# Half of one batch's q load moved behind four DMA transposes, and two key tiles rectified on VectorE, in a linear-attention and routed-MoE kernel

## The chip, the core and the metric

The kernel runs on one core of one Trainium2 chip. The metric is the device time of one execution in microseconds, as a median over runs. A NeuronCore has TensorE (PE, matmuls; PEld is its weight load), VectorE (DVE), ScalarE (ACT), GpSimd (POOL) and the sync engine (SP). Each takes its instructions in the order in which they were written. Work between engines is ordered by semaphores alone. Sixteen DMA engines move data for all queues; here POOL issues the loads from HBM, and SP issues the transposing copies.

## What is computed

The reference has two parts. The first is a linear attention over 8 batches of 8 heads, 576 positions and a head size of 64; the second a mixture of 8 experts, whose gate is balanced by 8 rounds of row and column normalisation.

```python
r = np.maximum(x, 0.0)                       # phi: of q and of k
phi = np.concatenate([r * c, r * s], -1)     # c, s: cos, sin of the position
kv  = np.einsum('bhsf,bhsd->bhfd', k_p, v)
z   = np.sum(k_p, axis=2)
num = np.einsum('bhsf,bhfd->bhsd', q_p, kv)
den = np.einsum('bhsf,bhf->bhs', q_p, z)[..., None] + 1e-06
x   = num / den                              # (4608, 512) over all heads
...
h = np.maximum(x @ w1[e], 0.0)               # for each expert e
out += P[:, e:e+1] * (h @ w2[e])             # P: the balanced gate
```

## The kernel before

The first 170 us or so hold the attention, with expert 0 laid between its pieces so that TensorE always has matmuls to do. The rest is the balancing and experts 1 to 7. The change is in the attention part.

One batch is handled as four pairs of heads, `hk` 0 to 3. In what follows (b, hk) is the pair hk of batch b, and batches count from 0, so the "second batch" is b = 1 and the "fourth" b = 3. A load (`load`, L201) brings one half of a batch, that is two pairs, of q, k or v: 288 KB, issued on POOL's queue, into one of four buffers for each name. With `held_back` the load also waits for the last VectorE instruction written before it.

For each pair the following is done:

- `prep_k` rectifies k in place, on ACT or, with `by_scalar=False`, on DVE. `prep_kp` multiplies it by cos and sin (DVE, `k_p`), and `prep_v` copies v next to a column of ones (DVE or ACT; the destination is borrowed room in `acc_lo`).
- `prep_q` rectifies q (DVE, `q_ld`) and multiplies it by cos and sin into one of three `q_p` buffers (DVE). From batch 2 on, a DMA transpose (L360, on SP's queue) then writes `q_pT`. For batches 0 and 1, TensorE transposes in `turn`.
- `sums` makes kv and z on PE (`small_ps<-acc_lo,k_p`), and its results are copied by ACT (`kv_sb`) and DVE (`zsel`).
- `denominators` multiplies all four transposed q of a batch by `zsel` on PE, 24 short matmuls, pair after pair. DVE then makes `den`, its reciprocal, `hi` and `hl`.
- `attend` spreads `hl` on PE (into `small_ps`), ACT copies it to `rb`, PE makes the numerator, and DVE multiplies the two into `xT`. There are four `small_ps` banks, and one `attend` uses four. So the second spread of the next `attend` waits for ACT to have read the last one, and its numerator waits for DVE's `xT`.

Expert 0 runs over blocks `j` of 512 tokens with 16 slots each: 8 slots of the first matmul (`ffn1`, `h_ps`, ACT writes `hT`) and 8 half slots of the second (`ffn2`, `y_ps`, ACT copies to `acc_lo`). A table written by hand, `at(block, slot, fn, ...)`, lays the attention's steps behind the slots; nothing reorders it. Block 0 finishes batch 1 and prepares the q of batch 2. Block 1 computes the sums, denominators and `attend` of batch 2, and prepares batch 3. Ahead of the blocks, a loop over `hk` runs `attend(0, hk)` between the first matmuls of expert 0 and prepares batch 1's k.

What the change touches, by the profile's line numbers: the first loop (L625 to L643), the loads of batch 3 (block 0, slot 13: L673 and L674; block 1, slot 0: L683 to L685) and the table of batch 3's preparation in block 1 (L704 to L708), put in place at L717. The k and v loads of batch 3 already stand at block 1, slot 0, behind the DVE work of that slot.

In block 1 the order on ACT around the change is: `hT` of slot 7, the two `k_ld` of (3,0) and (3,1), the copy of `y_ps`, and then the `rb` copies of `attend(2, 0)`. The order on DVE is: `q_ld` and `q_p` of (3,0), (3,1) and (3,2), then `den` to `hl` of batch 2, then `xT`.

Of the kernel before, what the change touches and what calls it, by code (L numbers as in the profile page):

```python
# [25 lines left out]
def kernel(  # L26
# [91 lines left out]
    te, ve, se = bound  # L118
# [62 lines left out]
    with ExitStack() as p1:  # L181
# [156 lines left out]
        def prep_k(b, hk, by_scalar=True):  # L338
            k16 = loaded["k", b, hk]
            if b and by_scalar:  # L340
                se.activation(out=k16, in_=k16, func=AF.Relu)
            else:
                ve.tensor_scalar(out=k16, in0=k16, scalar1=0.0, scalar2=None, op0=ALU.max)
# [27 lines left out]
        def prep_kp(b, hk):  # L371
            k16 = loaded.pop(("k", b, hk))
            k_p = kp_pool.tile([P, C, 2, D], F16, name="k_p")
            ve.tensor_tensor(
                out=k_p[:], in0=k16.unsqueeze(2).to_broadcast([P, C, 2, D]),
                in1=cs, op=ALU.mult,
            )
            kps[b, hk] = (
                k_p, v_augs[(b * HK + hk) % len(v_augs)] if b else loaded.pop(("v", b, hk))
            )  # L380
# [146 lines left out]
        def attend(b, hk):  # L527

            parts = ((0, 2 * C3), (2 * C3, C))
            rb_ps = [ps_s.tile([P, 512], FP32, name="small_ps") for _ in parts]  # L530
            rb = rb_pool.tile([P, C * HP], FP32, name="rb")
            for i, (c0, c1) in enumerate(parts):
                for j in range(c0 // C3, c1 // C3):
                    te.matmul(
                        out=rb_ps[i][:, (j * C3 - c0) * HP : ((j + 1) * C3 - c0) * HP],
                        lhsT=spread[0:96, j, hk].rearrange("p hh d -> p (hh d)"),
                        rhs=hls[b][:],
                        start=True,
                        stop=True,
                    )  # L540
                se.copy(out=rb[:, c0 * HP : c1 * HP], in_=rb_ps[i][:, 0 : (c1 - c0) * HP])
            num_ps = [ps_s.tile([P, 512], FP32, name="small_ps") for _ in parts]
            for i, (c0, c1) in enumerate(parts):
                for hh in range(2):
                    te.matmul(
                        out=num_ps[i][hh * HP : (hh + 1) * HP, 0 : (c1 - c0) * HP],
                        lhsT=kvs[b][0][:, hk, hh, :],
                        rhs=qTs[b, hk][:, c0:c1, hh * HP : (hh + 1) * HP],
                        start=True,
                        stop=True,  # L550
                    )
                ve.tensor_tensor(
                    out=xT[:, hk, b * S + c0 * HP : b * S + c1 * HP],
                    in0=num_ps[i][:, 0 : (c1 - c0) * HP],
                    in1=rb[:, c0 * HP : c1 * HP],
                    op=ALU.mult,
                )
# [25 lines left out]
        def at(block, slot, fn, *args):  # L583
            todo.setdefault((block, slot), []).append((fn, args))
# [39 lines left out]
        ]  # L624
        for hk in range(HK):  # L625
            attend(0, hk)
            if hk == 3:
                prep_k(1, 3)
            for kt in ((), (0,), (1,), (2, 3))[hk]:
                for ft, h_ps in enumerate(first_ps):  # L630
                    te.matmul(
                        out=h_ps[:],
                        lhsT=w0[0][:, kt, ft * P : (ft + 1) * P],
                        rhs=xT[:, kt, 0:TCH],
                        start=(kt == 0),
                        stop=(kt == KT - 1),
                    )
                    if kt == KT - 1:
                        se.activation(out=hT[:, ft, 0:TCH], in_=h_ps[:], func=AF.Relu)
            for i in ((), (0,), (1, 2), ())[hk]:  # L640
                prep_k(1, i)
            for i in ((), (0,), (1,), (2, 3))[hk]:
                prep_kp(1, i)  # L643
        for hk in range(3):
            prep_q(1, hk)

        for j in range(B):
            b = j + 1
            if j == 0:

                def sums_first(half):
                    sums_made(1, half, sums_begun(1, half))

                for hk in range(HK):
                    for i in range(3):
                        at(0, (5, 6, 6, 7)[hk], turn, 1, hk, i, i != 1)
                    if hk == 0:
                        at(0, 5, prep_q, 1, 3)
                    if hk == 2:
                        at(0, 6, prep_v, 1, 0, se.copy)  # L660
                        at(0, 6, prep_v, 1, 2, ve.tensor_copy)
                    if hk == 3:
                        at(0, 7, prep_v, 1, 1, se.copy)
                        at(0, 7, prep_v, 1, 3, ve.tensor_copy)
                for half in range(2):
                    at(0, 7, sums_first, half)
                at(0, 8, denominators, 1)
                at(0, 10, gates, 0)
                for hk in range(HK):
                    at(0, 11 + hk, attend, 1, hk)  # L670
            elif b < B:
                if j == 1:
                    for half in range(2):  # L673
                        at(0, 13, load, b + 1, half, "q", True)  # L674
                    for hk in range(HK):
                        if hk >= 2:
                            at(j, 0, prep_k, b, hk, False)
                        at(j, 0, prep_kp, b, hk)
                        at(
                            j, (0, 0, 1, 3)[hk], prep_v, b, hk,  # L680
                            (ve.tensor_copy, se.copy)[hk // 2],
                        )
                    for name in "kv":  # L683
                        for half in range(2):
                            at(j, 0, load, b + 1, half, name, True)  # L685
                    at(j, 3, sums, b, 0)
                    at(j, 5, sums, b, 1)
                else:
                    at(j, 0, sums, b, 1)
                at(j, 6 if j == 1 else 3, denominators, b)  # L690
                for hk in range(HK):
                    at(j, (9, 10, 12, 13)[hk] if j == 1 else 6 + 2 * hk, attend, b, hk)
            if j:
                at(j, 5, gates, j)
            if j == 0:
                for half in range(2):
                    at(j, 3, load, b + 1, half)
                for slot, fn, hk, *args in (
                    (8, prep_q, 0), (11, prep_k, 0), (12, prep_q, 1), (12, prep_k, 1),
                    (13, prep_q, 2), (14, prep_q, 3),  # L700
                ):
                    at(j, slot, fn, b + 1, hk, *args)
            elif b + 1 < B:
                for slot, fn, hk in (  # L704
                    (4, prep_q, 0), (5, prep_q, 1), (5, prep_q, 2), (7, prep_k, 0),
                    (8, prep_k, 1), (10, prep_kv, 0), (10, prep_k, 2), (12, prep_q, 3),
                    (12, prep_kv, 1), (12, prep_k, 3), (13, prep_kv, 2), (14, prep_kv, 3),
                ) if j == 1 else (  # L708
                    (4, prep_q, 0), (5, prep_k, 0), (5, prep_q, 1), (6, prep_k, 1),
                    (7, prep_q, 2), (8, prep_kv, 0), (8, prep_k, 2), (9, prep_q, 3),  # L710
                    (10, prep_k, 3), (10, prep_kv, 1), (12, prep_kv, 2), (13, prep_kv, 3),
                ) if j == 2 else (
                    (3, prep_k, 0), (4, prep_q, 0), (4, prep_k, 1), (5, prep_q, 1),
                    (7, prep_kv, 0), (7, prep_k, 2), (7, prep_q, 2), (9, prep_q, 3),
                    (9, prep_k, 3), (9, prep_kv, 1), (11, prep_kv, 2), (13, prep_kv, 3),
                ):
                    at(j, slot, fn, b + 1, hk)  # L717
                at(j, 15 if j == 1 else 14, sums, b + 1, 0)
            if j == 1:
                for name in "qkv":  # L720
                    for half in range(2):
                        at(j, 12, load, b + 2, half, name, True)
            elif j and b + 2 < B:
                for half in range(2):
                    at(j, 11 + half, load, b + 2, half, "qkv", True)
# [438 lines left out]
    for e in range(1, E):  # L1164
        if e == 2:
            se = nc.scalar
# [49 lines left out]
    while stream:  # L1216
        _, pair, name = stream.pop(0)
# [32 lines left out]
```

## Time and profile before

| what | value |
|---|---|
| median of 6 runs | 983.25 us (982.97 to 984.49) |
| the profiled execution | 982.97 us, span 981.3 us |
| PE busy | 966.2 us, 98% of the span |
| DVE busy | 806.7 us, 82% |
| ACT busy | 565.6 us, 58% |
| POOL busy | 60.7 us, 6% |
| granted TensorE clock | 1.0 |
| loads of q, 16 issues of 288 KB | median 6.6 us from issue to landing |
| loads of k, 16 issues of 288 KB | median 7.9 us |
| transposes into `q_pT`, 18 issues | median 3.8 us |
| PE's longest wait for a DMA | 1.7 us, once, for `q_pT<-q_p` |

The span is the time from the first to the last profiled instruction, and 1.7 us of the execution lie around it. The first five of the page's 40 slices, of 24.5 us each, show the DMA engines busy for nine tenths or more and the sixth for eight; later slices show seven tenths at most.

### The profile page before, as it was taken

How to read it: one execution, taken by the hardware profiler on the slowest of the kernel's cores; microseconds unless marked ns; L12 is line 12 of the kernel's file. 1: busy time of each engine (PE TensorE's matmuls, PEld its weight loads, DVE VectorE, ACT ScalarE, POOL GpSimd, SP SyncE). 2: the span in 40 equal slices, each digit the busy share in tenths (PEclk: the TensorE clock that was granted, in tenths of full speed). 3: DMA queues.
4: the chain of work that ended last, by engine and by line, in shares of the span. 5: the costliest groups of instructions: out<-in, count | busy, mean ns of one | idle time of the engine just before them, and what ended most of it. 6: DMA issues, size and time to landing. Idle time of an engine off the chain costs nothing.

```text
span 981.3 us, 20268 instructions
## 1 busy us (share of the span) xinstructions
PE 966.2 (98%) x7871; PEld 674.0 (69%) x7871; DVE 806.7 (82%) x1833; ACT 565.6 (58%) x1263; POOL 60.7 (6%) x82
## 2 busy tenths in 40 slices
PE   9999999989999999999999999999999999999997
PEld 6544454457777777777777777777777777777775
DVE  6767774789889888988788888988888888988887
ACT  6766665467776555555555555555555555555551
POOL 6221110010000000000000000000000000000001
PEclk9999999999999999999999999999999999999999
DMA  9999981740113400223103400223103401104435
GB/s 162 185 158 166 152 139 21 146 70 33 42 33 68 92 25 25 57 62 68 49 25 68 92 25 26 63 58 66 48 25 72 89 25 34 41 26 119 127 87 129
DMA packets 80336, 73.54 MB, mean 75 GB/s; under 512 B 33264, under 2 KB 72176, under 8 KB 80240
## 3 DMA queue, kind: packets, MB, share of 16 engines
q0 software_dynamic: 27232, 30.94, 20.2%
q1 hardware_dynamic: 52768, 41.06, 17.1%
q8 instruction: 61, 1.00, 0.4%
q14 instruction: 35, 0.29, 0.1%
q10 hardware_dynamic: 240, 0.26, 0.1%
HBM read 83.12 MB, written 12.98 MB: 98 GB/s over the span
## 4 chain that ended last, share of the span: by engine, by line
PE 92%; DVE 3%; DMA 2%; ACT 2%; POOL 1%; issue 1%; POOLq 0%; DVEq 0%; ACTq 0%; SPq 0%
PE rows_ps L109 34%; PE h_ps L109 27%; PE copied_ps L109 11%; PE p_ps L109 11%; PE y_ps L109 5%; PE small_ps L109 3%; DMA q_pT<-q_p 1%; DMA k_ld<-in_k_dram 1%; ACT hT L109 0%; DVE den L109 0%; DVE xT L109 0%; DVE acc_hi L923 0%; POOL hs_last L938 0%; DVE P_tok L109 0%; DVE k_p L109 0%
## 5 line engine op out<-in xcount | busy, mean ns | idle before, releaser
L923 DVE SCALAR_TENSOR_TENSOR acc_lo<-rows_ps,P_tok,acc_lo 128x512 f32<-128x512 f32 (+1 forms) x322 | 203.1, 639 | 74.8 <-PE rows_ps L109 74.7
L109 PEld LDWEIGHTS <-H 128*128 128x128 f16 x2080 | 203.0, 98 | 83.1 <-issue 1.2
L859 ACT CAST u<-h_ps 128x384 f16<-128x384 f32 x288 | 137.8, 478 | 131.1 <-PE h_ps L109 131.1
L109 PEld LDWEIGHTS <-w1e 128*128 128x128 f16 x1632 | 156.5, 98 | 66.5 <-issue 6.4
L853 DVE CUSTOM_DVE_ANT_0 H<-p_ps,u 128x384 f16<-128x384 f32 x329 | 180.8, 550 | 6.7 <-PE p_ps L109 6.5
L109 PEld LDWEIGHTS <-hs 128*128 128x128 f16 x1500 | 146.6, 98 | 56.2
L109 PE MATMUL h_ps<-S,w1e 128*128 128x384 f16 x672 | 164.1, 326 | 1.1 <-ACT u L109 0.9
L109 PE MATMUL p_ps<-xT,T 128*128 128x384 f16 x672 | 164.1, 326 | 0.1
L109 PE MATMUL rows_ps<-V,H 128*128 128x256 f16 x1000 | 150.0, 273 | 0.7 <-DVE acc_hi L923 0.7
L109 PE MATMUL h_ps<-xT,w1e 128*128 128x384 f16 (+1 forms) x616 | 150.0, 350 | 0.2 <-DVE xT L109 0.2
L109 PE MATMUL rows_ps<-w2e,hs 128*128 128x256 f16 x1000 | 150.0, 273 | 0.0
L891 ACT ACTIVATE H<-h_ps 128x384 f16<-128x384 f32 x144 | 70.7, 491 | 95.0 <-PE h_ps L109 95.0
L109 PEld LDWEIGHTS <-T 128*128 128x128 f16 x1008 | 98.1, 98 | 29.2 <-issue 2.7
L109 PE MATMUL rows_ps<-w2e,H 128*128 128x256 f16 (+1 forms) x568 | 91.2, 285 | 0.0
L872 ACT COPY copied_ps<-h_ps 128x384 f32<-128x384 f32 x144 | 67.5, 468 | 35.1 <-PE h_ps L109 35.1
L882 ACT ACTIVATE H<-copied_ps 128x384 f16<-128x384 f32 x144 | 70.9, 492 | 20.3 <-PE copied_ps L109 20.3
L109 PE MATMUL h_ps<-S,T 128*128 128x384 f16 x336 | 81.8, 325 | 0.3 <-ACT copied_ps L109 0.3
L109 PE MATMUL copied_ps<-xT,w1e 128*128 128x384 f16 x336 | 82.1, 326 | 0.0
L109 PE MATMUL copied_ps<-w2e,H 128*128 128x256 f16 x504 | 75.5, 272 | 0.0
L109 PE MATMUL rows_ps<-V,hs 128*128 128x256 f16 x500 | 75.0, 272 | 0.0
L923 DVE SCALAR_TENSOR_TENSOR acc_lo<-copied_ps,P_tok,acc_lo 128x256 f32<-128x256 f32 x126 | 60.0, 476 | 0.4
L923 DVE SCALAR_TENSOR_TENSOR acc_hi<-rows_ps,P_tok,acc_hi 128x512 f32<-128x512 f32 (+1 forms) x56 | 41.3, 737 | 20.5 <-PE rows_ps L109 19.7
(147 smaller groups left out, 948.8 us busy)
## 6 DMA issues: line engine op xcount, KB each, us to landing
S<-x_saved SPq DMA_DIRECT2D x108, 192.0 KB, 2.4
out_dram<-acc_lo SPq DMA_DIRECT2D x62, 128.0 KB, 2.4
w1e<-in_moe_w_dram POOLq DMA_DIRECT2D x7, 1024.0 KB, 8.9
w2e<-in_moe_w_dram POOLq DMA_DIRECT2D x7, 1024.0 KB, 9.7
q_ld<-in_q_dram POOLq DMA_DIRECT2D x16, 288.0 KB, 6.6
k_ld<-in_k_dram POOLq DMA_DIRECT2D x16, 288.0 KB, 7.9
v_ld<-in_v_dram POOLq DMA_DIRECT2D x16, 288.0 KB, 9.2
x_saved<-S SPq DMA_DIRECT2D x18, 192.0 KB, 1.9
```

The costliest lines, as they stand in the source:

```text
L109: i = getattr(self.engine, name)(*args, **kwargs)
L853: latest = ve._custom_dve(TENSOR_ADD_SAT, out=out, in0=ps[:, 0:TU], in1=t[:], s0=FP32_MAX, s1=0.0)
L859: se.copy(out=t[:], in_=ps[:, 0:TU])
L872: se.copy(out=Y[:, 0:TU], in_=X[:, 0:TU])
L882: se.activation(out=h11, in_=Y[:, 0:TU], func=AF.Relu)
L891: se.activation(out=h12, in_=X[:, 0:TU], func=AF.Relu)
L923: ve.scalar_tensor_tensor(out=a, in0=rows, scalar=P_tok[:, g, self.e : self.e + 1], in1=a, op0=ALU.mult, op1=ALU.add,)
```

## The change

Four things are edited.

- The q load of batch 3 at block 0, slot 13 brings only the first half, the pairs 0 and 1. The second half is issued at block 1, slot 0, ahead of the k and v loads there. So it comes after the last of batch 2's four transposes.
- In block 1 the preparation of q for (3,2) moves from slot 5 to slot 8. On DVE it then stands behind `den` to `hl` of batch 2.
- The copy of v for (3,3) at slot 14 goes from DVE to ACT.
- In the first loop (1,2) and (1,3) of k are rectified by DVE and no longer by ACT, and that of (1,3) is written later.

The instructions of PE and their order are the same in both kernels. SP issues the same transposes in the same order.

```diff
             attend(0, hk)
-            if hk == 3:
-                prep_k(1, 3)
...
             for i in ((), (0,), (1, 2), ())[hk]:
-                prep_k(1, i)
+                prep_k(1, i, i < 2)
             for i in ((), (0,), (1,), (2, 3))[hk]:
+                if i == 3:
+                    prep_k(1, i, False)
                 prep_kp(1, i)
...
                 if j == 1:
-                    for half in range(2):
-                        at(0, 13, load, b + 1, half, "q", True)
+                    at(0, 13, load, b + 1, 0, "q", True)
...
-                    for name in "kv":
-                        for half in range(2):
-                            at(j, 0, load, b + 1, half, name, True)
+                    for name, half in (("q", 1), ("k", 0), ("k", 1), ("v", 0), ("v", 1)):
+                        at(j, 0, load, b + 1, half, name, True)
...
-                    (4, prep_q, 0), (5, prep_q, 1), (5, prep_q, 2), (7, prep_k, 0),
+                    (4, prep_q, 0), (5, prep_q, 1), (7, prep_k, 0), (8, prep_q, 2),
                     (8, prep_k, 1), (10, prep_kv, 0), (10, prep_k, 2), (12, prep_q, 3),
-                    (12, prep_kv, 1), (12, prep_k, 3), (13, prep_kv, 2), (14, prep_kv, 3),
+                    (12, prep_kv, 1), (12, prep_k, 3), (13, prep_kv, 2), (14, prep_kp, 3),
+                    (14, prep_v, 3),
...
-                    at(j, slot, fn, b + 1, hk)
+                    at(j, slot, fn, b + 1, hk, *((se.copy,) if fn is prep_v else ()))
```

## The prediction

> **What bounds the kernel now.** I read the busy times first, then PE's waits, then the chain of waits around the transposes, then the timeline of 50 to 70 us. The busy times:
>
> ```profile
> PE 966.2 (98%) x7871; PEld 674.0 (69%) x7871; DVE 806.7 (82%) x1833; ACT 565.6 (58%) x1263; POOL 60.7 (6%) x82
> ```
>
> PE is busy for 98% of the span and its instructions don't change, so the change can only touch PE's idle time. PE's waits name one for a DMA, and the chain (start, length, what) passes through that transfer:
>
> ```profile
> PE small_ps L109 <- DMA q_pT<-q_p: 1.7, 1, 1.7
> ...
> 47.14 8.76 DMA q_pT<-q_p
> ...
> 55.98 0.76 DVE q_p L109
> 56.74 0.28 DVE den L109
> ```
>
> The transfer is the transpose of (2,3): issued at 47.14, landed at 55.90, where the median transpose takes 3.8 us. The q loads of batch 3 were issued in the same moments, so they shared the DMA engines with it. The timeline shows the rest (start, us, engine, shapes, in brackets the idle time and who ended it):
>
> ```profile
> 45.44 1.43 POOL L201 DMA_DIRECT2D q_ld<-in_q_dram  x2 [12.62 <-DVE q_p L109]
> 45.78 0.48 DVE L109 TENSOR_SCALAR q_ld<-q_ld 128x576 f16<-128x576 f16 x1
> ...
> 51.67 1.43 POOL L201 DMA_DIRECT2D k_ld<-in_k_dram  x2 [4.81 <-ACT hT L109]
> ...
> 55.02 0.31 DVE L109 TENSOR_SCALAR q_ld<-q_ld 128x576 f16<-128x576 f16 x1 [1.00 <-DMA q_ld<-in_q_dram]
> 55.93 0.35 PE L109 MATMUL small_ps<-q_pT,zsel 128*32 128x192 f16 x6 [1.72 <-DMA q_pT<-q_p]
> ...
> 57.28 0.60 ACT L109 ACTIVATE hT<-h_ps 128x512 f16<-128x512 f32 x1 [3.04 <-PE h_ps L109]
> 57.78 1.25 ACT L109 ACTIVATE k_ld<-k_ld 128x576 f16<-128x576 f16 x2
> ...
> 59.19 0.42 PE L109 MATMUL small_ps<-hl,acc_hi 96*128 96x192 f16 x3 [0.21 <-DVE hl L109]
> ...
> 60.07 0.82 DVE L109 TENSOR_TENSOR xT<-small_ps,rb 128x384 f16<-128x384 f32 x2 [0.94 <-ACT rb L109]
> ...
> 61.12 0.44 PE L109 MATMUL small_ps<-q_pT,kv_sb 128*64 128x384 f16 x4
> ...
> 69.81 0.46 PE L109 MATMUL small_ps<-acc_lo,k_p 64*128 64x65 f16 x18 [0.35 <-DVE acc_lo L109]
> ```
>
> PE idles 1.72 us at 54.21, 0.21 us before 59.19 and 0.35 us before 69.81: 2.28 us together. That is all the change can win here.
>
> **The change part by part, against this execution (982.97 us, span 981.3).**
>
> *The transpose of (2,3).* One load of the two goes from in front of it. Between 36 and 38 us loads alone move 210 GB/s, so 294,912 bytes are 1.40 us: landing at 54.5, a wait of 0.3 us left. The upper gain: in 53.50 to 54.20 the engines moved only 20 GB/s, an empty stretch that need not come again; with that the landing is at 53 or earlier. PE asks at 54.21, so 1.4 to 1.72 us come back. I take 1.72.
>
> *`prep_q` of (3,2) behind `hl`.* It now stands between PE's end at 56.18 and `den`, which started at 56.66 behind `q_p`. An earlier `den` began 0.04 us after its matmuls (36.00 to 36.04), so 0.44 us of the DVE chain go, and the wait of 0.21 us before 59.19 with them. Its own 0.31 + 0.76 us fit into DVE's 0.94 us of idle time before `xT`, nearly. So up to here PE is 1.72 + 0.21 = 1.93 us early.
>
> *What the moved load pushes back.* This decides. On POOL's queue the second q half now goes out ahead of k. Its last wait is the `k_p` that ends at 51.13, and POOL started 0.31 us after such an end in two other places (45.13 to 45.44, 66.97 to 67.28): 51.44, as against 51.67 for k before. The first k half follows 0.71 us later, at 52.15, second in line, and both v halves slip by half a microsecond. How long does a second load in line take? The trace has five:
>
> ```profile
> DMA to landing us min/median/max: 6.1/6.1/6.1
> ...
> DMA to landing us min/median/max: 6.4/6.4/6.4
> ...
> DMA to landing us min/median/max: 8.9/8.9/8.9
> ```
>
> These are the second loads issued at 67.99, 52.38 and 46.15; those at 85.63 and 106.14 took 6.3 and 5.7. The 8.9 had the transposes beside it, and so may this one, since SP issues (3,0) at 52.74. Bounds for the landing of k: 57.85 (5.7) and 61.05 (8.9). I take 6.05, between 5.7 and 6.4, so 58.2. Before, it landed at 51.67 + 5.3 = 57.0 and ACT took it at 57.78 without a wait.
>
> Behind that `k_ld` on ACT stand the second `k_ld`, the copy of `y_ps` and `rb`, without a gap: 57.78 to 60.07 is 2.29 us from `k_ld` to `xT`. The first half of `xT` takes 0.56 us and PE's numerator of (2,1) waits for it, with 0.05 us for the semaphore. So that numerator starts no earlier than landing + 2.90. In the kernel before it started at 61.12, held by PE itself. PE, 1.93 us early, asks at 59.19. With k at 58.2 it starts at 61.10: the whole gain is gone but 0.02 us, as ACT's wait for k has taken the place of PE's wait for the transpose. Each microsecond of k's landing is a microsecond of PE, from 56.3 (nothing lost) upward.
>
> The second q half itself is first in line; such loads took 4.1 to 6.1 us, so it lands at 55.5 to 57.5, and DVE wants it at 57.2. That costs 0 to 0.3 us, hidden under ACT's wait. The first v half, fourth in line, is wanted at about 63.1 and has landed by then if 9.6 us, the longest v load nearby, holds (53.6 + 9.6 = 63.2).
>
> *`prep_v` of (3,3) on ACT.* DVE sets the end of block 1: from the `xT` at 64.11 to the last v copy at 69.75 it hardly idles, and PE waits 0.35 us for that copy. Without it DVE ends with `k_p` at 69.39. ACT has 1.26 us idle before 67.46 and needs 0.70. Gain 0.35; without ACT's gap it would be nothing.
>
> *Two k on VectorE.* ACT loses two `k_ld` of 0.70 us. One stood at 23.50 with 0.52 us of idle time behind it, so worth nothing; the other delayed `rb` to 22.93 by some 0.15 us. DVE gains two operations, 0.30 us each by its k rows at 49.03 and 50.04. The first stands ahead of the `k_p` at 22.50, which overlaps it by 0.08 us as neighbours do here, so the `xT` that started at 23.44 after 0.18 us of idle time starts at 23.40 (-0.04). If the rectifying takes 0.48, as the one at 45.78 did while POOL was issuing, it is 23.58 (+0.14). The second delays batch 1's `q_p` by 0.3 us, which DVE has back in its 0.50 us idle before 30.06. I take +0.05.
>
> The row of 0.48 us bears on a rule that speaks against this part. The Trainium skill (SBUF — State Buffer, "Who interferes with whom") says that VectorE in a mode with two ports and GpSimd lock each other out for a whole instruction. By it, the relu at 22.5, which meets POOL's issue of 22.20 to 22.91, pays the 0.14; by the row of 0.30 the part would gain 0.04. Another rule would turn the main result. The same skill (DMA: Bandwidth & Descriptors, "Anatomy of one DMA") fits a POOL load as 2.0 us plus the bytes over 436 GB/s. By it q and k together would take 3.4 us from 51.44 and k land at 54.8, ACT would wait for nothing, and the sum would be -2.2 us. No load between 20 and 110 us, not even a first in line, came under 4.1 us, so I follow the rows.
>
> *Sum.* -1.72 - 0.21 + 1.91 (given back) - 0.35 + 0.05 = -0.32 us: 982.65 for this execution. The median of the runs is 0.28 above it, so 982.9.
>
> **Rivals.**
>
> *The gain stays.* With no load in front, the DMA engines may be empty when q and k come, and k lands by 56.5. For it: the first load in line at 105.43 took 4.1 us. Against: every second load took 5.7 or more. It gives -1.93 - 0.35 + 0.05 = -2.2: 981.0.
>
> *Slower: k behind q and the transposes of batch 3.* Place: ACT's `k_ld` of (3,0). Above a landing at 58.5 the kernel is slower than before, above 60.5 by more than 0.2%. With 8.9 us it lands at 61.05, the numerator starts at 63.95 instead of 61.12, +2.83 - 0.35 + 0.05 = +2.5: 985.8. For it: the transposes of (3,0) and (3,1) took 11.2 and 9.1 us among these loads. Against: k issued at 52.38 among the same took 6.4.
>
> *It doesn't do what it says.* The half that stays still runs ahead of the transpose, or the empty stretch comes again, and PE waits 0.3 to 1.7 us at 54.21. The wait for k then hides behind it: with 58.2 the numerator is at 61.1 all the same, and the time is 982.9 too, with 0.2 either way.
>
> **How the numbers follow.** Forecast 0.55, the gain stays 0.16, slower 0.17, not as it says 0.12. The forecast's own range, with k at 57.6 to 59.4, is 982.3 to 984.1. The whole range must leave out no more than 2 in 10: down to 980.9 it takes in the kept gain, up to 985.6 most of the slower case. This kernel's runs tell apart about 0.2%, or 2.0 us. Faster by more than that is the kept gain, 0.16; slower by more the second rival, 0.17; within it the other two, 0.67.
>
> **What would show it.** The wait of 1.7 us for `q_pT<-q_p` is gone from PE, and the transpose of (2,3) takes under 7 us. A new wait on ACT, `k_ld` for DMA `k_ld`, of about 2 us stands near 56 to 58. The `rb` after it starts near 60, and PE waits about 1.9 us in `small_ps` before 61.1 for ACT or DVE. PE's 0.35 us for `acc_lo` near 69 is gone or for another releaser. The forecast is wrong if k's first half lands before 57 or after 60, or if any PE wait after 75 us differs.

## The result, and the profile after

| kernel | median us | lowest to highest | runs | ratio to the kernel before, 95% interval |
|---|---|---|---|---|
| before | 983.07 | 982.41 to 984.58 | 37 | |
| changed | 987.12 | 982.05 to 988.23 | 16 | 1.0037 (1.003 to 1.0043) |

The change makes the kernel slower: by 0.37% in the ratio of the table, by 4.05 us (0.41%) between the medians. One of the 16 executions took 982.05 us and the other 15 took 985.48 or more, so the loss is not in every execution; no profile shows one without it. The prediction was 982.9 us with a range of 980.9 to 985.6: the time lies outside of the range. The profiled execution of the changed kernel took 985.02 us, span 983.3, and is one of its milder ones; a second profile of the same kernel, taken later, shows 986.37 us and is read with the experiments.

The first line is the busy times of the changed kernel (us, share of the span, instructions):

```profile
PE 967.9 (98%) x7871; PEld 674.6 (69%) x7871; DVE 806.7 (82%) x1834; ACT 565.0 (57%) x1262; POOL 60.7 (6%) x82
```

PE's instructions are as many as before, and still busy 98% of the span. So again only idle time and the clock can differ. PE's waits between 50 and 72 us, which held one wait of 1.7 us for `q_pT<-q_p` before, are now these (engine, group, releaser: us in total, times, longest):

```profile
PE small_ps L109 <- ACT rb L109: 2.3, 2, 1.4
PE small_ps L109 <- DVE xT L109: 0.5, 1, 0.5
```

The wait for the transpose is gone. Two waits for `rb`, which is ACT's copy in `attend`, have come, and one for DVE's `xT`. The timeline of the changed kernel tells what ACT itself waited for (start, us, engine, shapes, in brackets the idle time and who ended it):

```profile
51.12 0.71 POOL L201 DMA_DIRECT2D q_ld<-in_q_dram  x1 [5.28 <-DVE zsel L109]
51.83 1.44 POOL L201 DMA_DIRECT2D k_ld<-in_k_dram  x2
53.25 1.46 POOL L201 DMA_DIRECT2D v_ld<-in_v_dram  x2
...
54.10 0.35 DVE L109 TENSOR_SCALAR den<-small_ps 96x192 f32<-96x192 f32 x1 [0.55 <-PE small_ps L109]
...
57.17 1.26 ACT L109 ACTIVATE k_ld<-k_ld 128x576 f16<-128x576 f16 x2 [1.52 <-DMA k_ld<-in_k_dram]
...
59.92 0.54 PE L109 MATMUL small_ps<-q_pT,kv_sb 128*64 128x384 f16 x4
...
63.67 0.68 ACT L109 ACTIVATE k_ld<-k_ld 128x576 f16<-128x576 f16 x1 [3.27 <-DMA k_ld<-in_k_dram]
...
65.26 0.46 PE L109 MATMUL small_ps<-hl,acc_hi 96*128 96x192 f16 x3 [1.38 <-ACT rb L109]
65.27 0.45 DVE L109 COPY acc_lo<-v_ld 128x576 f16<-128x576 f16 x1 [3.40 <-DMA v_ld<-in_v_dram]
...
66.24 0.69 PE L109 MATMUL small_ps<-q_pT,kv_sb 128*64 128x384 f16 x4 [0.52 <-DVE xT L109]
66.86 3.09 PE L109 MATMUL y_ps<-w2e,hT 128*128 128x512 f16 x8
```

Up to 59.92 the kernel runs ahead: `den` starts 2.56 us earlier than before (54.10 against 56.66), and the numerator of `attend(2, 1)` 1.20 us earlier (59.92 against 61.12). Then the second k half comes late. ACT waits 3.27 us for it, until 63.67. The copy of `y_ps` and the `rb` of `attend(2, 2)` are queued behind it, and PE, whose next spread in `attend(2, 3)` waits for that copy, idles for 1.38 us. DVE waits 3.40 us for the first v half, with the `xT` behind it that PE waits 0.52 us for. The eight `y_ps` matmuls after that take 3.09 us where eight took 1.90 elsewhere: the granted clock was 0.5 for 3.41 us from 65.9.

The landings of the two k loads (issued at 51.83 and 52.54) and of the two v loads, in the changed kernel, from the answers on these tiles in this stretch:

```profile
  ACT k_ld L109: 4.8, 2
...
DMA to landing us min/median/max: 5.3/8.2/11.1
...
  DVE acc_lo L109: 3.4, 1
...
DMA to landing us min/median/max: 12.0/12.5/13.1
```

The first k half took 5.3 us, the second 11.1; in the kernel before these were 5.3 and 6.4. The v halves took 12.0 and 13.1, before 9.0 and 9.6. What lay beside them is on SP's queue: the transposes of (3,0) and (3,1), issued at 52.35 and 53.75.

```profile
L360 SPq DMA_TRANSPOSE q_pT<-q_p x2: 1302/3412/5521, 52.3 to 53.8; - x2
...
DMA to landing us min/median/max: 11.6/12.7/13.9
```

The same two in the kernel before were issued at 52.74 and 55.89. The first of them stood behind the transpose of (2,3), which landed only at 55.90; in the changed kernel that one has landed by 53.58. The packets of SP's queue agree: after those of batch 2's four transposes the next ones start at 57.48 us in the kernel before and at 56.44 in the changed one. So the issue of a transpose is not yet its transfer. By stretches, the changed kernel and then the kernel before (window; us; busy us of PE, PEld, DVE, ACT and POOL with their instructions; granted clock; DMA share, summed over queues; GB/s):

```profile
54.00:58.00 4.00, 4.00 (x25) 1.72 (x23) 3.35 (x6) 1.42 (x3) 0.71 (x1) 1.00 1.31 186
58.00:62.00 4.00, 2.93 (x17) 1.37 (x16) 2.31 (x5) 2.20 (x6) 0.00 (x0) 1.00 1.58 108
62.00:66.00 4.00, 2.34 (x16) 1.03 (x15) 0.73 (x2) 2.33 (x6) 0.00 (x0) 0.99 1.06 151
66.00:70.00 4.00, 3.76 (x20) 1.36 (x21) 3.97 (x10) 1.77 (x6) 1.21 (x2) 0.59 0.99 173
```

```profile
58.00:62.00 4.00, 3.79 (x26) 1.59 (x25) 2.22 (x6) 3.12 (x8) 0.00 (x0) 1.00 1.27 167
62.00:66.00 4.00, 4.00 (x28) 1.82 (x27) 3.37 (x9) 3.29 (x8) 0.00 (x0) 1.00 1.10 205
```

In 58 to 62 us the DMA engines are occupied more (1.58 against 1.27) and move less (108 GB/s against 167). That is where the loads lose much of their time.

Matching PE's instructions one by one in the two traces gives the ledger of starts, changed minus before: -2.21 us at the old 55.93, -2.55 at 59.19, -1.20 at 61.12, +0.45 at 64.81, +1.09 at 65.15, +2.52 at 66.83, +2.02 at 69.81, and +2.0 at the end. So a gain of 2.55 us is made, 1.35 of it is returned to the first k half, 2.29 go by the second k half and the first v half (-1.20 to +1.09), and the stretch of half clock adds 1.43 (to +2.52). The 0.50 us won back come at 69.81, where the kernel before waited 0.35 us for the copy of v.

### The profile page after: what moved, and what is told of

Read it like the earlier page. It is cut to its first block, busy times and chain, and to the rows that moved or that the text cites. A ratio compares the mean times of both kernels' runs of the same rounds, so it can differ in the third digit from the quotient of the medians.

```text
span 983.3 us, 20270 instructions
## 1 busy us (share of the span) xinstructions
PE 967.9 (98%) x7871; PEld 674.6 (69%) x7871; DVE 806.7 (82%) x1834; ACT 565.0 (57%) x1262; POOL 60.7 (6%) x82
## 4 chain that ended last, share of the span: by engine, by line
PE 90%; DMA 4%; issue 2%; DVE 2%; ACT 1%; POOL 1%; POOLq 0%; ACTq 0%; SPq 0%
PE rows_ps L109 34%; PE h_ps L109 27%; PE copied_ps L109 11%; PE p_ps L109 11%; PE y_ps L109 4%; PE small_ps L109 3%; DMA k_ld<-in_k_dram 2%; DMA w1e<-in_moe_w_dram 1%; DMA w2e<-in_moe_w_dram 1%; POOL q_ld L201 0%; DVE acc_hi L922 0%; POOL hs_last L937 0%; DVE P_tok L109 0%; DMA out_dram<-acc_lo 0%; DVE colp L109 0%
```

## The experiments

The theory after this reading: the loads of batch 3 lose their time to the transposes of batch 3, which now start beside them. Rivals: one of the other three edits does it; the place in the line of loads does it by itself; the clock does it.

The table gathers the landings. Each entry for a load is the time from issue to landing in us, from the profile of each kernel; "(3,0)" is issue and landing of that transpose. For the kernel that issues its loads in another order, "third" is the third in line.

| kernel | (3,0) | first in line | second | third | fourth | time us |
|---|---|---|---|---|---|---|
| changed | 52.35 to 63.92 | q 4.4 | k 5.3 | k 11.1 | v 12.0 | 987.12 |
| changed, second profile | 52.61 to 67.92 | q 4.4 | k 6.7 | k 12.9 | v 13.9 | 986.37, one execution |
| load move alone | 52.69 to 66.87 | q 4.6 | k 5.4 | k 12.7 | v 13.9 | 987.10 |
| k first | 52.40 to 67.64 | k 4.4 | k 6.1 | q 12.7 | v 13.9 | 990.55 |
| (3,1), (3,2) held | 52.45 to 65.95 | q 5.1 | k 6.8 | k 12.2 | v 12.7 | 986.25 |
| (3,0) held to 55.8 | 55.88 to 63.53 | q 4.6 | k 5.4 | k 7.1 | v 7.3 | 982.28 |
| all held to 61 | 61.05 to 64.42 | q 4.5 | k 5.2 | k 7.3 | v 7.6 | 982.08 |

### One edit at a time

The kernel before with the move of the loads alone:

```diff
-                    for half in range(2):
-                        at(0, 13, load, b + 1, half, "q", True)
+                    at(0, 13, load, b + 1, 0, "q", True)
...
-                    for name in "kv":
-                        for half in range(2):
-                            at(j, 0, load, b + 1, half, name, True)
+                    for name, half in (("q", 1), ("k", 0), ("k", 1), ("v", 0), ("v", 1)):
+                        at(j, 0, load, b + 1, half, name, True)
```

> The kernel before with the move of the second q half alone. Late loads (theory: the k and v loads of batch 3 now run beside batch 3's own transposes, ACT and DVE wait for them in front of rb and xT, PE waits behind these, and its granted clock falls): 985 to 988 us, the second k half takes 9 us or more to land, a clock under 1.000. Rival 'VectorE': the two k on DVE cost it, so without them the time is 982.4 or less. Rival 'slots': the moved q preparation and the v copy on ACT cost it; again 982.4 or less here.

Measured: 987.10 us (986.64 to 987.76, 5 runs), before 983.04, ratio 1.0041 (1.0028 to 1.0053). The move of the loads carries the whole loss. Its waits are partly others: `prep_q` of (3,2) still stands in front of `den`, DVE waits 2.0 us there for the second q half, and PE 2.5 us for `hl`. But the second k half takes 12.7 us as well. The granted clock fell here too, to 0.5 for 3.41 us from 60.62.

The kernel before with two k rectified by VectorE alone:

```diff
-                prep_k(1, i)
+                prep_k(1, i, i < 2)
...
+                if i == 3:
+                    prep_k(1, i, False)
                 prep_kp(1, i)
```

> The kernel before with the two k of batch 1 on VectorE alone. Late loads: 982.8 to 983.2 us, within 0.03% of before, clock 1.000. Rival 'VectorE': 985 us or more.

Measured: 983.33 us (982.94 to 984.99, 11 runs), ratio 1.0005 (0.9996 to 1.0014). It cannot be told from no change.

The kernel before with `prep_q` of (3,2) at slot 8 and the copy of v for (3,3) on ACT:

```diff
-                    (4, prep_q, 0), (5, prep_q, 1), (5, prep_q, 2), (7, prep_k, 0),
+                    (4, prep_q, 0), (5, prep_q, 1), (7, prep_k, 0), (8, prep_q, 2),
...
-                    (12, prep_kv, 1), (12, prep_k, 3), (13, prep_kv, 2), (14, prep_kv, 3),
+                    (12, prep_kv, 1), (12, prep_k, 3), (13, prep_kv, 2), (14, prep_kp, 3),
+                    (14, prep_v, 3),
...
-                    at(j, slot, fn, b + 1, hk)
+                    at(j, slot, fn, b + 1, hk, *((se.copy,) if fn is prep_v else ()))
```

> The kernel before with q's preparation of (3,2) behind hl and the v copy of (3,3) on ACT alone, both q loads where they were. Late loads: the waits of 0.21 and 0.35 us go, 1.72 stays: 982.3 to 982.8 us. Rival 'slots': 985 us or more.

Measured: 982.72 us (981.90 to 984.31, 11 runs), ratio 0.9998 (0.9989 to 1.0007). The times tell nothing apart, but the trace does: PE's waits for `hl` (0.21) and `acc_lo` (0.35) are gone, the 1.8 us for the transpose are still there, and PE runs 0.42 us ahead after `hl`, of which 0.15 lie ahead of batch 2 already, and 0.79 after 69.8. At that place both steps are worth about what they were priced at (0.27 for 0.21, 0.37 for 0.35).

### Taking the transposes away from the loads

The changed kernel with (3,0), (3,1) and (3,2) held on SP until the first v half of batch 3 has landed; nothing else differs:

```diff
-                nc.sync.dma_start(
+                i = nc.sync.dma_start(
                     out=qTs[b, hk], in_=q_p[:].rearrange("p c a d -> p (c a d)"),
                     transpose=True,
                 )
+                if b == 3 and hk < 3:
+                    after(issued["v", 3, 0], i)
```

> The changed kernel, with batch 3's first three transposes held on SP until the first v half of batch 3 has landed; the loads stay as changed. If the transposes beside the loads delay them: the second k half lands within 7.5 us of its issue (11.1 in the changed kernel), ACT's wait of 3.3 us for it is under 1 us, PE has no wait over 1 us behind it, clock 1.000, 980.5 to 982.0 us. Rival 'the line alone': five loads in one line are late by their number; then the second k half still takes over 10 us and the time is 985 or more.

Measured: 982.08 us (981.71 to 983.10, 11 runs), ratio 0.9991 (0.9982 to 1.0). The whole loss is gone, though the time is a little above the 980.5 to 982.0 that were expected. The five loads in the same line now take 4.5, 5.2, 7.3, 7.6 and 8.3 us, and each transpose 3.3 to 3.4 once it is let go. So the second k half loses about a microsecond by being third in line and no longer second as in the kernel before (7.3 against 6.4), and the remaining 3.8 to 5.5 to the transposes beside it (11.1 to 12.9 against 7.3).

How many transposes does it take? The same with (3,1) and (3,2) held, (3,0) free:

```diff
-                if b == 3 and hk < 3:
+                if b == 3 and hk in (1, 2):
```

> The changed kernel with batch 3's transposes (3,1) and (3,2) held on SP until the first v half of batch 3 has landed; (3,0) goes out when it likes, as in the changed kernel. It asks how many transposes beside the loads it takes. Theory 'each transpose in flight costs the loads its share': one transpose of 288 KB beside the line of five loads, so the second k half lands between the 59.95 of the run with all three held and the 63.65 of the changed kernel, near 61 to 62; the waits of ACT for it and of DVE for the first v half shrink to 0.5 to 1.5 us each, PE loses 0.8 to 1.8 us near 58 to 66, and the time is 982.5 to 984.5. Rival 'one transpose beside the loads is enough to stall them': second k half at 63 or later, waits of 3 us, time 986 to 988. Rival 'the late loads are not (3,0)'s doing at all': the same times as with all three held, second k half at 60.0, first v half within 8 us, time 982.0 to 982.5.

Measured: 986.25 us (984.55 to 986.98, 6 runs), ratio 1.0029 (1.0016 to 1.0041), second k half 12.2 us. This is the rival's outcome: my theory that each transpose costs the loads its own share has fallen. One transpose in the line is enough. (In its profiled execution the granted clock was also 0.5 for 3.41 us, from 61.87.)

And does it matter when that one starts? Only (3,0) is held, until the second q half has landed; the others are free behind it:

```diff
-                if b == 3 and hk < 3:
-                    after(issued["v", 3, 0], i)
+                if b == 3 and hk == 0:
+                    after(issued["q", 3, 1], i)
```

> The changed kernel with only the transpose (3,0) held on SP, until the second q half of batch 3 has landed (about 55.6), with the other three free behind it in SP's queue. In the kernel before, SP's queue was taken by the transpose of (2,3) until 55.9, so that nothing of (3,0) could move ahead of that, and there the second k half took 6.4 us; in the changed kernel (2,3) is through at 53.6. Theory 'the transpose of (2,3) was the shelter of the k loads: three microseconds of head start decide': with (3,0) no sooner than 55.6 the second k half lands at 59.5 to 61.5 instead of 63.65 to 65.55, ACT's wait for it is under 1.5 us, the v halves are still late (first v half 62.5 to 65, DVE waits 0.5 to 2.5 us), and the time is 982.5 to 985. Rival 'any transpose beside the third load stalls it, whenever it starts': second k half at 63 or later, 986 to 988. Rival 'v was the smaller matter': v within 9 us, time 982.0 to 982.5.

Measured: 982.28 us (981.28 to 984.17, 10 runs), ratio 0.9995 (0.9985 to 1.0004): below the time that the theory gave, with the second k half where it put it (59.65) and v better than it put it. With v within 9 us, time and v are those of the last rival. Landings of k and v in this kernel, and the two transposes that were issued at 55.88 and 58.58:

```profile
  ACT k_ld L109: 1.6, 1
...
DMA to landing us min/median/max: 5.4/6.2/7.1
...
DMA to landing us min/median/max: 7.3/7.9/8.6
...
L362 SPq DMA_TRANSPOSE q_pT<-q_p x2: 2598/3273/3948, 55.9 to 58.6; - x2
...
DMA to landing us min/median/max: 6.0/6.8/7.7
```

The transpose (3,0) is issued 3.53 us later than in the changed kernel (55.88 against 52.35) and lands 0.39 us earlier (63.53 against 63.92); the first v half lands 4.67 us earlier (60.58 against 65.25). What the two queues moved from 56 to 60 us tells why. q0 carries POOL's loads and q1 SP's transposes (packets, MB, share of 16 engines' time). First the kernel before, then the changed kernel, then the one with (3,0) held to 55.8:

```profile
q0 software_dynamic: 671, 0.72, 105.0%
q1 hardware_dynamic: 325, 0.08, 15.1%
```

```profile
q0 software_dynamic: 265, 0.28, 79.0%
q1 hardware_dynamic: 1005, 0.26, 65.4%
```

```profile
q0 software_dynamic: 668, 0.72, 116.7%
...
q1 hardware_dynamic: 3, 0.00, 0.1%
```

With the hold, (3,0) is issued at 55.88, but its packets start only at 59.85, when the second k half has landed (59.65). So the loads of k have the engines to themselves. In the changed kernel the transposes move 0.26 MB there, the loads lose 0.44 MB against the kernel with the hold, and both together move less (0.54 MB against 0.72). So the loss goes with the sharing, and the moment of the issue decides whether the k loads share at all.

In the kernel before, (2,3) kept (3,0) back: its packets start at 57.48, move 0.08 MB by 60 us, and its k loads were through by 58.8. The change took part of that shelter away when it made (2,3) faster, and lengthened the line of loads. How much of the loss is due to the start 1.04 us earlier (56.44 against 57.48) isn't shown, as the hold to 55.8 starts the packets later than the kernel before did. Nor is sharing always as dear: from 58 to 61 us the two queues moved 0.46 and 0.11 MB side by side in the kernel before, 0.24 and 0.05 in the changed one. What makes that difference stays open.

### Is it the clock, or the order of the loads?

Ten dead matmuls keep PE busy in its idle places of `attend`; the output doesn't use them:

```diff
+        def fill(n):
+            bank = ps_h[0].tile([P, TCH], FP32, name="h_ps")
+            for _ in range(n):
+                te.matmul(
+                    out=bank[:], lhsT=ones_sq[:],
+                    rhs=ones_sq[:, 0:1].to_broadcast([P, TCH]), start=True, stop=True,
+                )
...
+                    at(j, 10, fill, 4)
+                    at(j, 13, fill, 6)
```

> The changed kernel with ten matmuls of ones that nobody reads put on PE in front of two spreads that wait there, four before attend(2,1) and six before attend(2,3). They take 0.21 us each at full clock, 2.1 us together, and lie in waits of 0.94 and 1.38 us in the changed kernel's profile. If the fall of the granted clock is a cost of its own: clock 0.999 to 1.000 and 983.4 to 985.5 us, under the changed kernel's 987.1 although PE has more to do. If the waits alone make the time: 987 or more, as the dead matmuls can only add.

Measured: 987.00 us (985.53 to 988.10, 5 runs), ratio 1.0038 (1.0026 to 1.0051). That is no gain, and the outcome that was named for the waits alone. In its profiled execution the clock was 1.0 throughout and the time 986.32: the loss is there without any fall of the clock.

The changed kernel once more, unedited:

> The changed kernel once more, unedited. Its profiled execution took 985.02 us, 2.1 us under the median of its timed runs, so the profile may show a mild case. If landings vary from run to run: here too the second k half lands third in line, between 63 and 66 us, and the execution is 985 to 988 us; a landing near 65.5 goes with a time of 986 us or more. If it is the clock alone: the landing is 63.65 within 0.3 us and a longer time goes with more stretches of a clock under 1.

Measured: 986.37 us, clock 1.0 over the whole span. The second k half lands at 65.55, the first at 58.73 (6.7 us). PE in that stretch:

```profile
60.91 0.46 PE L109 MATMUL small_ps<-hl,acc_hi 96*128 96x192 f16 x3 [2.35 <-ACT rb L109]
61.50 0.54 PE L109 MATMUL small_ps<-q_pT,kv_sb 128*64 128x384 f16 x4
...
67.16 0.46 PE L109 MATMUL small_ps<-hl,acc_hi 96*128 96x192 f16 x3 [1.70 <-ACT rb L109]
68.29 0.54 PE L109 MATMUL small_ps<-q_pT,kv_sb 128*64 128x384 f16 x4 [0.67 <-DVE xT L109]
```

Against the kernel before, its starts are -2.38 us at the old 59.19, +0.46 at 61.31, +2.35 at 64.81 and +3.14 at 65.15, and +3.2 to +3.4 from there to the end. Here the wait for the first k half returns the gain (2.35), the second k half (1.70) and DVE's first v half (0.67) add the loss, and no clock is needed. This one execution is 3.24 us above the kernel before in the same runs (983.13), most of the timed loss of 4.05.

The changed kernel with both k halves ahead of the second q half:

```diff
-                    for name, half in (("q", 1), ("k", 0), ("k", 1), ("v", 0), ("v", 1)):
+                    for name, half in (("k", 0), ("k", 1), ("q", 1), ("v", 0), ("v", 1)):
```

> The changed kernel with both k halves ahead of the second q half in the line. Late loads: the k halves land as early as in the kernel before (first within 5.5, second within 6.5 us of issue) and ACT's long wait goes, but the second q half is now third and runs beside batch 3's transposes: over 7 us, DVE waits for it over 2 us in front of xT, and the time stays at 985 to 988 us. If only ACT's wait for k costs: 981 to 983 us.

Measured: 990.55 us (989.73 to 990.98, 5 runs), ratio 1.0073 (1.006 to 1.0085), worse than the 985 to 988 that were expected. PE's longest wait in this kernel, and DVE's behind it:

```profile
PE small_ps L109 <- DVE xT L109: 8.5, 1, 8.5
```

```profile
DVE q_ld L109 <- DMA q_ld<-in_q_dram: 9.0, 1, 9.0
```

The k halves land in 4.4 and 6.1 us, and now the q half, third in line, takes 12.7. Third place is the late one here too, though it holds q and not k. Part of the 990.55 us is the clock: it was 0.5 for 10.24 us from 60.58, and the eight `y_ps` matmuls behind PE's long wait took 3.35 us.

### A version that beats both

With the transposes of batch 3 held until the first v half, the kernel before (both q halves early) with the three small edits:

```diff
+                if b == 3 and hk < 3:
+                    after(issued["v", 3, 0], i)
```

> The kernel before with the two k, the slots and the held transposes of batch 3, but both q halves loaded where they were. This has all but the load's move. PE's wait of 1.7 us for the transpose of (2,3) is there again: 982.2 to 982.8 us. If the gain of 'held' came from holding the transposes alone and not from the load's move: 982.1 or less, with no such wait.

Measured: 982.54 us (981.79 to 984.63, 11 runs), ratio 0.9995 (0.9986 to 1.0004). PE's 1.6 us for the transpose of (2,3) are back.

The changed kernel, held, with k ahead of q and `prep_q` of (3,2) behind `attend(2, 1)`:

```diff
-                    for name, half in (("q", 1), ("k", 0), ("k", 1), ("v", 0), ("v", 1)):
+                    for name, half in (("k", 0), ("q", 1), ("k", 1), ("v", 0), ("v", 1)):
...
-                    (4, prep_q, 0), (5, prep_q, 1), (7, prep_k, 0), (8, prep_q, 2),
-                    (8, prep_k, 1), (10, prep_kv, 0), (10, prep_k, 2), (12, prep_q, 3),
+                    (4, prep_q, 0), (5, prep_q, 1), (7, prep_k, 0),
+                    (8, prep_k, 1), (10, prep_q, 2), (10, prep_kv, 0), (10, prep_k, 2), (12, prep_q, 3),
```

> 'held' with the first k half ahead of the second q half, and q's preparation of (3,2) behind attend(2,1). The first k half should land by 55.7, so ACT's wait of 1.4 us in 'held' goes and with it PE's 0.8 us: 981.0 to 981.6 us. If q or the second k half is late instead: 982 or more.

Measured: 982.37 us (981.69 to 983.74, 11 runs), ratio 0.9992 (0.9983 to 1.0001), above the 981.0 to 981.6 expected. No wait for `rb` is left, but a new one has come: the `q_p` of (3,3) needs the buffer of (3,0), whose transpose lands only at 64.05, and DVE waits 1.5 us. The last version lets (3,0) go after the second k half:

```diff
-                    after(issued["v", 3, 0], i)
+                    after(issued[("k", "v", "v")[hk], 3, (1, 0, 0)[hk]], i)
```

> The last version (k, q, k, v, v as the order of the five loads, prep_q of (3,2) behind attend(2,1), transposes of batch 3 held on SP) with an earlier release for the first transpose: (3,0) is held until the second k half has landed (about 58.5), (3,1) and (3,2) still until the first v half has (about 60.7). It is to free the q_p buffer that VectorE waited 1.5 us for. If the hold on the buffer is what remained: (3,0) lands by 62 to 62.5 instead of 64.05, DVE's wait for it is under 0.3 us, PE's waits near 66 to 68 for acc_lo and k_p (1.5 us together) are gone, and the time is 981.0 to 981.9. Rival 'a transpose beside the v loads slows both': the first v half lands after 63.5 and DVE waits 1 us or more for it, time 982.4 to 984.

Measured: 981.86 us (981.37 to 982.53, 11 runs), before 983.13 in the same runs, ratio 0.9987 (0.9978 to 0.9996). It is the only version here that is faster than the kernel before by its interval, by 1.3 us. The time is as expected, the reason only in part: the second k half lands at 60.03, so (3,0) goes out little earlier and lands at 64.06 as it did; DVE still waits 1.1 us for the buffer, and PE 1.14 us in three pieces. Why the time came down by 0.5 us against the last version isn't shown.

## Why the prediction was wrong, point by point

- *The transpose of (2,3): right.* It took 6.75 us instead of 8.76, PE's wait of 1.72 us is gone, and PE stands 2.21 us ahead at the old 55.93. With `hl` it is 2.55, priced at 1.93; 0.31 us of that lie ahead of batch 2 already, so 2.24 stand against the 1.93.
- *The first k half: right in its mechanism.* It was put at 58.2, with the numerator 2.90 us behind its landing. Measured: landing at 57.15, numerator at 59.92 (2.77 behind); in the second profile 58.73 and 61.50 (2.77). So the gain is given back where the text said, 1.35 us of it in one execution and all of it in the other. The landing of 57.15 is below the range of 57.6 to 59.4 that the text took. Its "five" second loads leave out a sixth in the same trace, issued at 125.78, which took 4.98 us.
- *The step that failed is "What the moved load pushes back", in what it leaves out.* It prices one load, the first k half, as second in line. The second k half, now third, got no price at all, and the v halves were let "slip by half a microsecond", with the first v half put at 63.2 by the 9.6 us of a v load nearby. Measured: 11.1 to 12.9 us for the second k half and 12.0 to 13.9 for the first v half, and behind them a loss of 2.3 us in one execution and 2.7 in the other. The third place by itself would have cost little: with the transposes held it took 7.3 us, and the time was 982.08. The cost that the sum lacks is that of the transposes beside the third to fifth loads.
- *The row that misled.* The text saw the danger and named it as its second rival: k behind q and the transposes of batch 3, 985.8 us with a chance of 0.17. It put it at the first k half, and set against it that "k issued at 52.38 among the same took 6.4". But this load was hardly among the same. The transpose (3,0), issued at 52.74, stood behind (2,3) until 55.89, and its packets moved from 57.48 on, 1.28 us ahead of that load's landing. The step that speeds up (2,3) removes part of that cover, and the sum never asked who else had been waiting behind it. Holding (3,0) to 55.88, so that its packets start at 59.85, gives 7.1 us and 982.28.
- *`prep_q` of (3,2) and the v copy on ACT: right* by the trace of the kernel that has these two alone (0.21 and 0.35 us of waits gone). *The two k:* the 0.05 us are below what the times can tell (ratio 1.0005, 0.9996 to 1.0014).
- *The clock:* the sum had no term for it. In the profiled execution it added some 1.4 us, in the second none. It isn't the cause of the loss: without any fall, that second profile took 986.37 us and the kernel with the dead matmuls 986.32.
- *The sum.* Of its terms -1.72, -0.21, +1.91, -0.35 and +0.05 only the 1.91 is far off: it stands for all that the loads give back. By the second profile's ledger that is 2.84 up to the numerator of `attend(2, 1)` (from -2.38 to +0.46) and 2.7 more by 65.15 (to +3.14), 5.5 together.

## What to carry to other kernels

When a transfer is made to land earlier, list what stood behind it in its own queue, and where those transfers will now run; the cover that a slow transfer gave to others is a term of the sum. Price every load of a line that is lengthened, not only the first one wanted. And if a row is used as evidence that neighbours do no harm, check that they were in fact moving: an issued transfer may move nothing for microseconds, and the packets of its queue show it.

## What the runs showed of the hardware

The moment at which a transpose is issued beside a line of loads decides more than how many are. With (3,0) issued between 52.35 and 52.69, about when the third load was, the third to fifth loads took 11.1 to 15.1 us in six profiles; issued at 55.88 or later, 7.1 to 8.6 in four. In the six the packets of batch 3's transposes began between 55.4 and 56.5 us, and the loads moved 0.28 to 0.49 MB from 56 to 60 us; with the hold to 55.8 and with all held, 0.72 and 0.76. The transpose itself gains nothing by its early start: it landed at 63.9 to 67.9 in the six, at 63.5 to 64.4 in the four. The Trainium skill (DMA: Bandwidth & Descriptors, "Rules for kernel authors") says that a transpose next to ordinary DMAs needs nothing. That rule is about data, and on the time it is silent; here, for the time, it is too little, where one hold on one transpose is worth 4.8 us (987.12 to 982.28). The same page ("Queues, rings and completion order") has each engine take turns between its queues packet by packet. An estimate from it: a transpose would cost the loads no more than its own time. That time is 3.3 to 3.4 us with all held, and with (3,0) alone in flight the third load lost 4.8 (12.17 against 7.33). Why the two together move less than the loads alone stays open; no run here takes it apart further.

The issue of a transpose can hold SP's queue: 5.5 and 6.1 us for (3,1) and (3,2) in the changed kernel, whose forerunners stood among the loads, but 1.3 us for (3,3), which was issued at 67.62, when (3,1) had landed and (3,2) had not (68.66).

The clock doesn't follow the idle time in a simple way. In the profiled execution of the changed kernel it fell to 0.5 for 3.41 us from 65.89, within the last of four waits of 0.94, 0.13, 1.38 and 0.52 us in 8 us; in the second profile waits of 2.35, 1.70 and 0.67 us, 4.7 in all against 3.0, left it at 1.0. The stretch at 0.5 was 3.41 us long in two other kernels as well (the load move alone; (3,1), (3,2) held), and 10.24 us, three times that, with k first. The Trainium skill (TensorE: Matmul & The Clock Gate, "Part 1: The HAM clock gate") gives a free-running window of 3413 ns. The length of the stretches agrees, and a window that runs free would explain that one execution falls and another not, which the two profiles alone don't prove.
